# Attention, a mixture of experts and a gated MLP in one kernel: small expert tiles as one stationary block, and engine orders from a second planning pass

## The chip, the cores and the metric

The kernel runs on one core of one Trainium2 chip. The metric is the device time of one execution in microseconds (us). The engines are PE (TensorE, matmuls), DVE (VectorE), ACT (ScalarE), POOL (GpSimd) and SP (the queue that issues most DMAs). PSUM, into which PE writes, has eight banks of 128 x 512 float32.

## The reference

Three stages in a row, all in float32, on 4 sequences of 576 tokens with 512 features (2304 tokens in all):

```
scores = q @ k.T / 8                                   # 32 heads of 576 x 64
attn   = softmax(where(scores >= rowmax - tau, scores, -1e9));  x = attn @ v
# experts: each token goes to one of 8, chosen by x @ w_gate and a local gate
out[b, s] = p[e] * (relu(x[b, s] @ w1[e]) @ w2[e])     # w1[e] 512 x 1024, w2[e] 1024 x 512
# gated MLP
h = gelu(x @ w_in);  u, v = halves of h
v_n = (v - mean(v)) / sqrt(var(v) + 1e-6) * g_ln
out = x + (u * (w_sg @ v_n + b_sg)) @ w_out
```

## The kernel before, in words

**Numbers in two parts.** From the experts on, a float32 operand is held as a high part, rounded to the type that PE takes at full speed, and a low part, the rest. A product is three matmuls: high x high, high x low, low x high. ACT writes the high part as a copy, DVE the low part as a difference.

**The expert stage** (`Tail.moe`). A first expert's first two tiles of 128 tokens come ahead (`plain`); then a loop over eight slots (`CAPS`, `SLOTS`) runs one expert each. Slot 0 has 272 tokens, slots 1 to 3 have 352, slot 4 has 240, and slots 5 to 7 have 192. For each slot SP loads eight pieces of weights of 512 KB; ACT (`whi`) and DVE (`wlo`) split them. The first layer (`L1`) has the weights stationary and the slot's tokens moving: eight groups of 12 matmuls. Relu gives the hidden layer, whose high part `hh` comes from ACT and low part `hl` from DVE. In the second layer (`second`, `L2`) a tile of 128 tokens of the hidden layer is stationary and the weights move, 512 columns at a time: 8 pieces x 3 products = 24 matmuls of 128x512 a tile. A slot's last tile may be a small one: 16 tokens in slot 0, 96 in slots 1 to 3, 112 in slot 4, 64 in slots 5 to 7. It takes 24 matmuls all the same. `put` copies the sum out of PSUM on ACT (`ysb`) and stores it to the DRAM tensor `ys` (`yst`).

**The end of the expert stage.** The small tile of slot 6 is held back: after slot 7's first tile come slot 6's small tile and slot 7's small tile, 48 matmuls. The MLP's first half (`p` = 0) gathers its tokens from `ys` with indirect DMAs on POOL's queue (`gth`). These wait for all stores but those of the last two small tiles.

**The MLP** (`Tail.mlp`) runs per half of the tokens: three groups of three tiles (`group`), then gates (`gate`: `sp`, then `fin`). In a group each tile is scaled by its expert's probability (`xpg`: on DVE in the first group, on ACT later), transposed (`xT`), split (`xh` ACT, `xl` DVE) and multiplied (`vp` 12 matmuls of 512 columns, `up` 12 of 384). Gelu alternates ACT and DVE: `sq`, `sqh`, `tanh`, `gelu`; the last one frees the PSUM bank. `bn`/`bna` (DVE) give mean and variance; 1/sqrt is a guess (`rq`, three DVE operations of 128x3) and three Newton steps (`rqn`, 13 POOL operations of 128x3). Then `vc` (DVE), `vh` (ACT) and `vl` (DVE) make the normalized halves that `sp` needs. `shi`/`slo` split the MLP's own weights.

**Who sets the order.** Every operation is recorded with an engine, a duration, the operations that it needs and a priority (`Graph.add`). `Graph.order` plays a greedy list schedule over all engines: on each engine the operation with the lowest (earliest start + priority) goes next. The order that comes out is the program order of each engine, in which every engine then runs strictly. It also picks PSUM banks: of those that are free, the one freed last.

```
k = s + alpha * o.prio
...
o.banks = [max((b for b in range(8) if bank[b] <= s), key=lambda b: (bank[b ^ 1] > s, bank[b]))]
```

From the expert stage on, nearly all instructions carry one line, L193, that of the recording helper; attention's have their own lines (L437 scores, L442 row maximum, L466 mask).

Of the kernel before, what the change touches and what calls it, by code (L numbers as in the profile page):

```python
# [8 lines left out]
F32 = mybir.dt.float32  # L9
# [15 lines left out]
class Op:  # L25
    __slots__ = ("eng", "dur", "deps", "emit", "prio", "start", "end", "n", "name", "need", "cls", "users", "banks", "fill", "lag")

    def __init__(self, eng, dur, prio, emit, name):
        self.eng, self.dur, self.prio, self.emit, self.name = eng, dur, prio, emit, name
        self.need, self.cls, self.users, self.banks, self.fill, self.lag = 0, None, [], None, False, 0.0  # L30


class Graph:
# [11 lines left out]
    GAP = 0.05  # L45

# [6 lines left out]
    def add(self, eng, dur, prio, emit, name, deps=()):  # L53
        o = Op(eng, dur, prio, emit, name)
        o.deps = [d for d in deps if d is not None]
        o.n = len(self.ops)
        self.ops.append(o)
        return o

    def order(self, alpha=1.0, smax=3):  # L60
# [27 lines left out]

        def when(o, f):
# [14 lines left out]
        while left:  # L104
            best = None
            for e, lst in ready.items():
                f = free.get(e, 0.0)
                c = cs = ck = None
                for o in lst:
                    s = when(o, f)  # L110
                    if s >= INF:
                        continue
                    k = s + alpha * o.prio
                    if c is None or (k, o.n) < (ck, c.n):
                        c, cs, ck = o, s, k
# [13 lines left out]
            o.start, o.end = s, s + o.dur + (self.STEP if e == "PE" else 0.0)  # L129
# [25 lines left out]
        return sorted(ops, key=lambda o: (o.start, o.n))  # L155

# [1166 lines left out]
class Tail:  # L1323
# [10 lines left out]
    CLAG = 2.0  # L1334
    IDLE = 0
# [43 lines left out]
    def moe(self, dep, x_dram, ys, side, sw):  # L1379
# [83 lines left out]
        def second(t, hh, hl, W8, hu, T, after=(), W=W, n=2, more=()):  # L1463
            p = Bank()
            for f0 in range(0, 8, n):
# [8 lines left out]
                R["last"] = g.op("PE", pe(512, 3 * n), W(T), mm, r=hu[f0:f0 + n] + (list(more[f0 + 1:f0 + n + 1])) + wc, deps=after, pw=p, name="L2")  # L1474
                R["last"].fill = n == 1
                T += pe(512, 3 * n)
            put(t, p, T)
            return T
# [44 lines left out]
        switch(*Mem.CELLS[3])  # L1523
        base, free, held = NA, [], None
        for k, cap in enumerate(CAPS):
# [18 lines left out]
            H = (self.HH, self.HL)  # L1544
            if k > 5:
                pitch = z
                H = tuple(self.HP + (2 * (k - 6) + i) * 8 * z for i in range(2))
            hh, hl = (self.M(a, [128, 8, pitch], F32R) for a in H)
            hu = [g.use(*[(a + pitch * m, pitch) for a in H]) for m in range(8)]
            if k == 0:  # L1550

                for x in (hh, hl):
                    g.op("POOL", 0.6, W(T + self.PZ), lambda x=x, a=z, b=pitch: nc.gpsimd.memset(x[:, :, a:b].bitcast(F32), 0.0), w=hu, name="half")
            free = []
            for m in range(8):
# [10 lines left out]
                first(m, p, hh, hl, z, hu[m], W(T + 1.3), W(T + 1.6))  # L1566
# [4 lines left out]
            def row(i, t, T, after, hh=hh, hl=hl, W8=W8, hu=hu, H=H, pitch=pitch):  # L1571
                if pitch % 128 and i:
                    flat = [self.M(a, [128, 8 * pitch + 64], F32R) for a in H]
                    x, y = (lambda f, a=a: a[:, f * pitch + 128:f * pitch + 256] for a in flat)
                    return second(t, x, y, W8, hu, T, after, more=hu + (follow if t == NT - 3 else []))
                c = slice(i * 128, (i + 1) * 128)
                return second(t, hh[:, :, c], hl[:, :, c], W8, hu, T, after)
# [4 lines left out]
            elif k == 7:  # L1582
                follow = hu[:1]
# [242 lines left out]
    def mlp(self, out):  # L1826
# [24 lines left out]
        def rsqrt(var2, q):  # L1851
# [17 lines left out]
            return y, guess, newton  # L1869

        def group(p, gi):
# [4 lines left out]
            for n, i in enumerate(turn):  # L1876
# [13 lines left out]
                for (k0, k1), xk in zip(parts[i], xt[i]):  # L1890
# [13 lines left out]
                    else:  # L1904
                        g.op("ACT", act(512), W(need - 4), lambda t=t, y=y: nc.scalar.activation(y, y, AF.Copy, scale=self.pg[p][:, t:t + 1]), r=[xu], w=[xu], deps=first, name="xpg")
# [7 lines left out]
            y, guess, newton = rsqrt(mv, rq)  # L1913
# [43 lines left out]
            g.op("POOL", 3.4, W(T[0] + 3), newton, r=[rq], w=[rq], name="rqn")  # L1957
# [224 lines left out]
```

## Time and profile before

| what | value |
|---|---|
| median of 3 runs | 772.18 us (771.45 to 773.78) |
| profiled execution, its own time | 771.32 us |
| its span in the profile | 769.5 us |
| PE busy | 747.7 us (97%) |
| DVE busy | 610.5 us (79%) |
| ACT busy | 456.4 us (59%) |
| POOL busy | 181.2 us (24%) |
| granted TensorE clock | 0.999 of full speed |

The profiled execution's own time is 1.8 us above its span, which covers first to last instruction. A busy share is an average over stages: attention fills about 0 to 300 us, the experts up to 540 us, the MLP the rest.

### The profile page before, as it was taken

The page shows a single profiled execution, that of the slowest core. Times are in us where ns is not written, and L with a number is a line of the kernel's source. Part 1 is how long each engine was busy: PE and PEld are TensorE (multiplying, and loading weights), DVE is VectorE, ACT ScalarE, POOL GpSimd, SP SyncE. Part 2 cuts the span into 40 slices and gives each one's busy share as a digit, 9 for nine tenths or more (in the row PEclk, how much of TensorE's full clock was granted, in tenths as well). Part 3 has the DMA queues.
Part 4 walks back from the last instruction along what each step waited for, and adds up shares of the span by engine and source line. Part 5 has one row for each costly group of instructions (what it writes and reads, how often), then busy time and mean ns, then how long its engine had stood idle before and what let it go on. Part 6 is the DMA issues. An engine that isn't in the chain of part 4 may idle for free.

```text
span 769.5 us, 13939 instructions
## 1 busy us (share of the span) xinstructions
PE 747.7 (97%) x4885; PEld 646.1 (84%) x4886; DVE 610.5 (79%) x1321; ACT 456.4 (59%) x842; POOL 181.2 (24%) x348
## 2 busy tenths in 40 slices
PE   8999999999999999999999999999899999999997
PEld 5787888788788678889898998998788898988996
DVE  7999999999889999667877868876698864588752
ACT  6888888888888585263544445643665542455410
POOL 6433353433344320320101100002241120122100
PEclk9999999999999999999999999999999999999999
DMA  7442323453231243698759578752710032200012
GB/s 217 134 128 63 127 78 127 167 179 126 78 127 63 91 163 117 202 299 295 244 189 289 175 239 296 235 194 92 207 41 1 1 110 69 70 1 0 15 42 69
DMA packets 46910, 103.13 MB, mean 134 GB/s; under 512 B 7540, under 2 KB 7540, under 8 KB 46836
## 3 DMA queue, kind: packets, MB, share of 16 engines
q1 hardware_dynamic: 43636, 91.72, 35.9%
q0 software_dynamic: 3200, 10.49, 4.6%
q8 instruction: 39, 0.64, 0.4%
q14 instruction: 35, 0.29, 0.1%
HBM read 80.17 MB, written 22.02 MB: 133 GB/s over the span
## 4 chain that ended last, share of the span: by engine, by line
PE 43%; DVE 6%; POOL 3%; ACT 2%; DMA 2%; issue 1%; POOLq 0%; ACTq 0%; DVEq 0%
PE PS L193 43%; DVE MF L193 3%; POOL rq L193 2%; DVE r L193 1%; ACT MF L193 1%; DMA MF<-ys,MF 1%; DVE bs L193 1%; POOL MF L193 1%; ACT r L193 1%; POOL r L193 0%; DVE MR L193 0%; DMA ys<-MF 0%; DMA out_dram<-MF 0%; ACT MR L193 0%; DVE rq L193 0%
## 5 line engine op out<-in xcount | busy, mean ns | idle before, releaser
L193 PE MATMUL PS<-r,r 128*128 128x512 f32 (+4 forms) x1544 | 302.2, 352 | 4.2 <-DVE MF L193 3.1
L193 PEld LDWEIGHTS PS<-r,r 128*128 128x128 f32 x1544 | 256.5, 188 | 35.2 <-DVE MF L193 4.0
L437 PE MATMUL PS<-MR 128*128 128x288 f32 x640 | 123.1, 322 | 5.2 <-DVE MF L466 3.2
L466 DVE SCALAR_TENSOR_TENSOR MF<-PS,MF 128x576 f32<-128x576 f32 x144 | 116.1, 811 | 7.8 <-ACT MF L457 6.1
L457 ACT ACTIVATE MF<-PS,MF 128x576 f32<-128x576 f32 x144 | 106.8, 751 | 16.4 <-DVE MF L442 9.4
L442 DVE TENSOR_REDUCE MF<-PS 128x1 f32<-128x576 f32 x144 | 106.1, 751 | 4.8 <-PE PS L437 3.6
L437 PEld LDWEIGHTS PS<-MR 128*128 128x128 f32 x640 | 93.2, 192 | 13.5 <-DVE MF L466 6.6
L193 PE MATMUL PS<-MR,r 128*128 128x256 f32 (+2 forms) x616 | 101.7, 322 | 0.9 <-DVE MF L193 0.9
L193 PEld LDWEIGHTS PS<-MR,r 128*128 128x128 f32 x616 | 91.3, 188 | 9.6 <-DVE MF L193 1.7
L379 ACT ACTIVATE c<-PS 128x512 f32<-128x512 f32 (+1 forms) x160 | 86.0, 564 | 17.5 <-PE PS L486 16.5
L193 ACT ACTIVATE r<-PS 128x512 fp32r<-128x512 f32 (+7 forms) x113 | 49.4, 451 | 79.0 <-PE PS L193 77.4
L486 PE MATMUL PS<-ident,MF 128*128 128x128 f32 x576 | 84.8, 274 | 2.2 <-ACT c L379 1.3
L193 ACT ACTIVATE MF<-PS 128x512 f32<-128x512 f32 (+1 forms) x64 | 35.7, 558 | 72.7 <-PE PS L193 61.3
L486 PEld LDWEIGHTS PS<-ident,MF 128*128 128x128 f32 x576 | 67.7, 140 | 5.9 <-ACT c L379 3.0
L193 DVE SCALAR_TENSOR_TENSOR MF<-MF,PS 128x384 f32<-128x384 f32 (+1 forms) x84 | 50.0, 605 | 19.0 <-ACT MF L193 18.2
L193 DVE TENSOR_TENSOR r<-c,r 128x1024 fp32r<-128x1024 f32 x46 | 55.2, 1222 | 10.2 <-ACT r L193 9.0
L452 POOL TENSOR_TENSOR MF<-MF,cf 128x1 f32<-128x1 f32 x120 | 28.2, 237 | 136.8 <-DVE MF L442 123.7
L193 POOL DMA_INDIRECT MF<-x_dram,inv x22 | 22.3, 1016 | 145.6 <-PE PS L193 117.0
L193 PE MATMUL PS<-r,MR 128*128 128x256 f32 (+3 forms) x384 | 52.4, 294 | 0.4 <-PEq L1777 0.4
L193 DVE SCALAR_TENSOR_TENSOR r<-PS,r 128x352 fp32r<-128x352 f32 (+4 forms) x72 | 30.7, 436 | 27.5 <-ACT r L193 26.8
L193 PEld LDWEIGHTS PS<-r,MR 128*128 128x128 f32 x384 | 50.7, 189 | 1.1 <-DVEq L1777 0.7
L193 ACT ACTIVATE r<-c 128x1024 fp32r<-128x1024 f32 x46 | 46.8, 1054 | 6.2 <-PE PS L193 5.7
(236 smaller groups left out, 935.5 us busy)
## 6 DMA issues: line engine op xcount, KB each, us to landing
c<-in_w_dram SPq DMA_DIRECT2D x64, 512.0 KB, 5.3
c<-in_kP_dram SPq DMA_DIRECT2D x32, 288.0 KB, 2.9
c<-in_qP_dram SPq DMA_DIRECT2D x32, 288.0 KB, 3.0
ys<-MF SPq DMA_DIRECT2D x36, 256.0 KB, 3.7
x_dram<-c SPq DMA_DIRECT2D x6, 768.0 KB, 4.3
MF<-in_w_in_dram SPq DMA_DIRECT2D x8, 512.0 KB, 4.5
c<-in_vP_dram SPq DMA_DIRECT2D x12, 320.0 KB, 4.6
out_dram<-MF SPq DMA_DIRECT2D x12, 256.0 KB, 2.0
```

The source lines that it names most:

```text
L193: return lambda *a, **k: x(*[v(y) for y in a], **{n: v(y) for n, y in k.items()})
L379: self.nc.scalar.activation(out, src, AF.Copy, **k)
L437: self.nc.tensor.matmul(self.PS[:, banks[hf], 0:288], q, k[:, 288 * hf:288 * hf + 288], start=(n == 0), stop=(n == len(ops) - 1))
L442: self.nc.vector.tensor_reduce(m, self.tl[i]["s"], axis=AX.XY, op=ALU.min)
L452: (self.nc.vector if eng == "DVE" else self.nc.gpsimd).tensor_tensor(self.nbt(i), self.tl[i]["m"], self.tp, op=ALU.add)
L457: self.nc.scalar.activation(e.rearrange("p (a b) -> p a b", a=2), t["s"], AF.Exp, bias=t["m"], scale=-1.0)
L466: self.nc.vector.scalar_tensor_tensor(w.rearrange("p (a b) -> p a b", a=2), t["s"], self.nbt(i), t["e"].rearrange("p (a b) -> p a b", a=2) ...
L486: self.nc.tensor.transpose(p[:, c, :], t["w"][:, z + c * 128:z + (c + 1) * 128], self.cst["ident"])
```

## The change

1. **Small tiles share stationary blocks.** Where the last tile's tokens, rounded up to a multiple of 32, are 64 or fewer (slots 0, 5, 6, 7), the hidden layer is laid out so that the small tile's high and low columns stand side by side (`both`). One stationary block holds high and low; the weights' high and low parts move through it. `narrow` does 16 matmuls a tile in place of 24, low x low now included. The two row groups of the result are added at the end: ACT copies the lower one (`ysb`), DVE adds the upper one (`ysa`, new, one a tile). `hl` of these slots becomes two DVE operations, one for the full tiles and one for the small one.
2. **Two planning passes.** `order` runs the old schedule once (`plan`), takes PE's order from it, gives each operation the latest time by which PE needs it or its bank (`aim`), and plans again. In the second pass PE's order from slot 0 on is fixed, the other engines' key there is the latest time, durations come from a new table (`TIME`), and DVE and POOL operations marked `SHARED` may not overlap. Banks from slot 0 on: the one that has been free longest. Attention keeps its key, but is planned again with the new durations.
3. **Newton steps.** In each half's third group they move from POOL (13 operations) to DVE (10). Elsewhere POOL keeps them and the plan's duration for them rises from 3.4 to 4.85 us. The plan adds 2 us for a gather before `xpg` on ACT (`XPL`).

```diff
+    TIME = {
+        ("ACT", "kh"): 0.668, ("ACT", "qh"): 0.668, ("ACT", "nb"): 0.19, ("ACT", "vh"): 0.663, ("ACT", "xpg"): 0.625,
...
-    def order(self, alpha=1.0, smax=3):
+    def plan(self, alpha=1.0, smax=3, line=None):
...
+        def key(o, s):
+            return s + alpha * o.prio if line is None or o.n < self.n0 or o.eng == "PE" else s + 14.8 + self.BETA * (o.late - o.step - 293.0)
+
         def when(o, f):
+            if line is not None and o.eng == "PE" and o.n >= self.n0 and line[pos[0]] is not o:
+                return INF
             t = max(f, at[o.n])
+            if line is not None and o.port:
+                t = max(t, held["POOL" if o.eng == "DVE" else "DVE"])
...
-                    o.banks = [max((b for b in range(8) if bank[b] <= s), key=lambda b: (bank[b ^ 1] > s, bank[b]))]
+                    can = [b for b in range(8) if bank[b] <= s]
+                    o.banks = [min(can, key=lambda b: bank[b]) if o.n >= self.n0 else max(can, key=lambda b: (bank[b ^ 1] > s, bank[b]))]
...
+    def aim(self, seq):
...
+        for o in reversed(seq):
+            o.late = min(o.late, free.get(o.n, INF), t + 5.0)
+            s = ideal[o.n] if o.eng == "PE" else o.late - o.step
+            for d in o.deps:
+                d.late = min(d.late, s - self.lat(d, o.eng) - o.lag)
+        return [o for o in line if o.n >= self.n0] + [None]
+
+    def order(self, alpha=1.0, smax=3):
+        return self.plan(alpha, smax, self.aim(self.plan(alpha, smax)))
...
+            if q:
+                g.op("DVE", dve(512), W(T), lambda: nc.vector.tensor_tensor(o[0:n], p.ap[0:n], o[0:n], op=ALU.add), w=[yo], r=[yo], pr=p, name="ysa")
...
+        def narrow(t, both, q, W8, hu, T, after):
+
+            p = Bank()
+            for f0 in range(0, 8, 2):
+                wc, wh, wl = W8[4 + f0 // 2]
+
+                def mm(f0=f0, wh=wh, wl=wl):
+                    for f in (f0, f0 + 1):
+                        for j, y in enumerate((wh, wl)):
+                            nc.tensor.matmul(p.ap[0:2 * q], both[:, f, :], y[:, f % 2 * 512:f % 2 * 512 + 512], start=(f == 0 and j == 0), stop=(f == 7 and j == 1))
...
+            full, q = z // 128 * 128, (z % 128 + 31) // 32 * 32
+            if q <= 64:
...
+                for c, hx, lx in ((slice(0, full), slice(0, full), hl), (slice(full, z), slice(0, z - full), both[:, :, q:2 * q] if q else None)):
+                    if c.stop > c.start:
+                        g.op("DVE", dve(c.stop - c.start), W(T + 1.6), lambda m=m, p=p, c=c, hx=hx, lx=lx, hh=hh: nc.vector.scalar_tensor_tensor(
+                            lx[:, m, hx], p.ap[:, c], 0.0, hh[:, m, c].bitcast(F32), op0=ALU.max, op1=ALU.subtract), r=[hu[m]], w=[hu[m]], pr=p, name="hl")
...
-            g.op("POOL", 3.4, W(T[0] + 3), newton, r=[rq], w=[rq], name="rqn")
+            if gi < 2:
+                g.op("POOL", 4.85, W(T[0] + 3), newton, r=[rq], w=[rq], name="rqn")
+            else:
+                g.op("DVE", 1.65, W(T[0] + 3), fast, r=[rq], w=[rq], name="rqd")
```

**PE at the end of the expert stage.** The rows are PE's program order before, from slot 7's last L1 matmuls (192 columns) over the three L2 tiles (512 columns), the MLP's first transposes (`ident`) and the first `vp` matmuls.

```order
L193 MATMUL PS<-r_3193,r_3113 128x192 x3
L193 MATMUL PS<-MR,r_3193 128x512 x24
L193 MATMUL PS<-r_3112,r_3193 128x512 x24
L193 MATMUL PS<-MR,r_3193 128x512 x24
L193 MATMUL PS<-ident,MF 128x128 x12
L193 MATMUL PS<-r_3112,r_3193 128x512 x6
L193 MATMUL PS<-r_2737,r_3193 128x512 x3
```

The same place now:

```order
L256 MATMUL PS<-r_3186,r_3113 128x192 x3
L256 MATMUL PS<-MR,r_3186 128x512 x24
L256 MATMUL PS<-r_3112,r_3186 128x512 x16
L256 MATMUL PS<-MR,r_3186 128x512 x16
L256 MATMUL PS<-ident,MF 128x128 x4
L256 MATMUL PS<-r_3112,r_3186 128x512 x6
L256 MATMUL PS<-ident,MF 128x128 x4
L256 MATMUL PS<-r_2733,r_3186 128x512 x3
```

The two small tiles have 16 matmuls each, and the transposes of the second and third tile now stand between the first `vp` matmuls.

**ACT at the start of the MLP.** Before; `MF<-PS` of 512 or 384 columns is `sq`, `MR<-c` is `shi`, `r<-PS` is `xh`. Of `MF<-MF 128x512` the first two are `xpg` of gathered tiles, then after `sq` one `xpg` and the first `tanh`, then after the next `sq` one `xpg` and the second `tanh`.

```order
L193 ACTIVATE r_3193<-PS 128x4x128 x2
L193 ACTIVATE MF<-MF 128x512 x2
L193 ACTIVATE MF<-PS 128x512
L193 ACTIVATE MF<-MF 128x512 x2
L193 ACTIVATE MR<-c_78 128x576
L193 ACTIVATE MF<-PS 128x512
L193 ACTIVATE MF<-MF 128x512 x2
L193 ACTIVATE MF<-PS 128x384
L193 ACTIVATE MR<-c_79 128x576
L193 ACTIVATE MF<-MF 128x384
```

Now; the second row is `sq`, the third the first `tanh`, and the three in one row are `xpg`, the second `tanh`, `xpg`. The single `MF<-MF 128x512` behind `shi` is the `xpg` that stood just ahead of the second `tanh`.

```order
L256 ACTIVATE r_3186<-PS 128x4x128 x2
L256 ACTIVATE MF<-PS 128x512
L256 ACTIVATE MF<-MF 128x512
L256 ACTIVATE MF<-PS 128x512
L256 ACTIVATE MF<-MF 128x512 x3
L256 ACTIVATE MF<-PS 128x384
L256 ACTIVATE MR<-c_80 128x576
L256 ACTIVATE MF<-MF 128x512
L256 ACTIVATE MF<-MF 128x384
```

Before, all four scalings stood ahead of the second `tanh`; now one does, and the other three follow it.

**DVE behind the guess of the second group, first half.** Before; `rq` is the guess, `MF<-MF,mv` is `vc`, `r<-MF,rq,r` is `vl`, which needs the Newton steps, `MF<-MF,PS` is `sqh` or `gelu`.

```order
L193 TENSOR_SCALAR rq_108<-rqi_109 128x3
L193 SCALAR_TENSOR_TENSOR MF<-MF,PS 128x512
L193 SCALAR_TENSOR_TENSOR MF<-MF,mv_101 128x512 x3
L193 SCALAR_TENSOR_TENSOR r_3193<-MF,rq_108,r_3193 128x512
L193 SCALAR_TENSOR_TENSOR MF<-MF,PS 128x512
L193 BN_STATS bs_97<-MF 128x6
```

Now; `MR<-c` is `slo`.

```order
L256 TENSOR_SCALAR rq_108<-rqi_109 128x3
L256 SCALAR_TENSOR_TENSOR MF<-MF,mv_101 128x512
L256 SCALAR_TENSOR_TENSOR MF<-MF,PS 128x384
L256 SCALAR_TENSOR_TENSOR MF<-MF,mv_101 128x512
L256 TENSOR_TENSOR MR<-c_79,MR 128x576
L256 TENSOR_TENSOR MR<-c_75,MR 128x576
L256 TENSOR_TENSOR MR<-c_77,MR 32x576
L256 SCALAR_TENSOR_TENSOR MF<-MF,PS 128x512
L256 SCALAR_TENSOR_TENSOR r_3186<-MF,rq_108,r_3186 128x512
```

Between guess and first `vl` stand four operations before, and one `gelu`, three `slo`, two `vc` and one `sqh` now.

## Rows read from the trace of the kernel before

**Rows 1.** The profile's page: busy us of each engine, share of span, instructions.

```profile
PE 747.7 (97%) x4885; PEld 646.1 (84%) x4886; DVE 610.5 (79%) x1321; ACT 456.4 (59%) x842; POOL 181.2 (24%) x348
```

**Rows 2.** Stage windows: length, busy us of each engine, granted clock, DMA share, GB/s.

```profile
100.00:200.00 100.00, 99.45 (x748) 82.18 (x749) 94.84 (x206) 85.03 (x164) 41.06 (x74) 1.00 0.41 133
...
450.00:529.00 79.00, 79.00 (x553) 72.68 (x553) 64.50 (x108) 41.25 (x70) 0.95 (x1) 1.00 0.63 213
...
541.00:598.00 57.00, 53.33 (x278) 47.45 (x279) 45.37 (x83) 36.67 (x65) 15.35 (x34) 1.00 0.25 74
...
646.00:705.00 59.00, 58.04 (x299) 50.79 (x298) 40.49 (x75) 30.65 (x54) 11.82 (x31) 1.00 0.13 41
```

**Rows 3.** Timeline of PE, end of the experts: start, us, instruction, idle time before.

```profile
528.68 5.63 PE L193 MATMUL PS<-r,r 128*128 128x512 f32 x24
534.14 5.76 PE L193 MATMUL PS<-MR,r 128*128 128x512 f32 x24
539.74 1.04 PE L193 MATMUL PS<-ident,MF 128*128 128x128 f32 x8
...
541.40 9.93 PE L193 MATMUL PS<-r,r 128*128 128x512 f32 x48
553.48 4.46 PE L193 MATMUL PS<-r,r 128*128 128x384 f32 x24 [2.15 <-DVE MF L193]
```

**Rows 4.** Timeline of POOL, the MLP's first and seventh gather.

```profile
532.77 0.95 POOL L193 DMA_INDIRECT MF<-ys,MF  x1 [70.25 <-DVE r L193]
...
544.19 0.96 POOL L193 DMA_INDIRECT MF<-ys,MF  x1 [0.52 <-issue]
```

**Rows 5.** Timeline of DVE: scaling of the MLP's first three gathered tiles.

```profile
536.13 0.62 DVE L193 TENSOR_SCALAR MF<-MF 128x256 f32<-128x256 f32 x2 [3.95 <-DMA MF<-ys,MF]
538.55 0.53 DVE L193 TENSOR_SCALAR MF<-MF 128x512 f32<-128x512 f32 x1 [1.80 <-DMA MF<-ys,MF]
540.21 0.72 DVE L193 TENSOR_SCALAR MF<-MF 128x512 f32<-128x512 f32 x1 [1.13 <-DMA MF<-ys,MF]
```

**Rows 6.** Timeline of ACT: the scaling of the seventh gather's tile, with `tanh` behind it.

```profile
551.46 1.24 ACT L193 ACTIVATE MF<-MF 128x512 f32<-128x512 f32 x2 [3.69 <-DMA MF<-ys,MF]
```

**Rows 7.** PE's waits, 545 to 615 and 0 to 300: us, times, longest.

```profile
PE PS L193 <- DVE MF L193: 3.4, 5, 2.2
PE PS L193 <- DVE r L193: 1.1, 1, 1.1
...
PE PS L437 <- DVE MF L466: 3.2, 6, 1.3
```

**Rows 8.** Timeline of POOL: Newton steps of the first half's first two groups.

```profile
566.85 0.19 POOL L193 TENSOR_TENSOR rq<-rq 128x3 f32<-128x3 f32 x1 [6.94 <-DVE rq L193]
...
573.78 0.24 POOL L193 TENSOR_SCALAR rq<-rq 128x3 f32<-128x3 f32 x1
588.95 0.20 POOL L193 TENSOR_TENSOR rq<-rq 128x3 f32<-128x3 f32 x1 [14.93 <-DVE rq L193]
...
590.26 0.58 POOL L193 TENSOR_TENSOR rq<-rq,rq 128x3 f32<-128x3 f32 x1
...
593.53 0.23 POOL L193 TENSOR_SCALAR rq<-rq 128x3 f32<-128x3 f32 x1
```

**Rows 9.** Timeline of DVE around the second group's Newton steps.

```profile
588.49 0.17 DVE L193 TENSOR_SCALAR rqi<-rq 128x3 int32<-128x3 int32 x1
...
589.37 2.07 DVE L193 SCALAR_TENSOR_TENSOR MF<-MF,mv 128x512 f32<-128x512 f32 x3
594.54 0.75 DVE L193 SCALAR_TENSOR_TENSOR r<-MF,rq,r 128x512 fp32r<-128x512 f32 x1 [3.10 <-ACT r L193]
```

**Rows 10.** DVE by shape, 300 to 769 us: count, busy us, mean ns, idle before.

```profile
L193 DVE TENSOR_TENSOR MF<-PS,MF 128x512 f32<-128x512 f32 x14 | 9.7, 691 | 13.7 <-PE PS L193 11.6 <-DMA out_dram<-MF 2.0
L193 DVE SCALAR_TENSOR_TENSOR r<-PS,r 128x192 fp32r<-128x192 f32 x24 | 8.5, 356 | 8.0 <-ACT r L193 7.5
...
L193 DVE SCALAR_TENSOR_TENSOR MF<-PS,MF 128x64 f32<-128x64 f32 x16 | 3.4, 215 | 0.0
```

More of the change, by code (lines that the diff above doesn't have):

```diff
@@ L25 @@
 class Op:
-    __slots__ = ("eng", "dur", "deps", "emit", "prio", "start", "end", "n", "name", "need", "cls", "users", "banks", "fill", "lag")
+    __slots__ = ("eng", "dur", "deps", "emit", "prio", "start", "end", "n", "name", "need", "cls", "users", "banks", "fill", "lag", "late", "port", "step")
     def __init__(self, eng, dur, prio, emit, name):
@@ L45 @@
     GAP = 0.05
+    BETA = 0.06
+    n0 = 1 << 30
+    TIME = {
+        ("ACT", "kh"): 0.668, ("ACT", "qh"): 0.668, ("ACT", "nb"): 0.19, ("ACT", "vh"): 0.663, ("ACT", "xpg"): 0.625,
+        ("DVE", "mask"): 0.739, ("DVE", "bn"): 0.714, ("DVE", "bna"): 0.147, ("DVE", "la"): 0.464, ("DVE", "rd"): 0.098,
+        ("DVE", "slo"): 1.135, ("DVE", "wlo"): 1.135, ("POOL", "nb"): 0.256, ("POOL", "half"): 0.786, ("POOL", "gth"): 0.982,
+        ("PE", "av"): 2.466, ("PE", "tr"): 0.42, ("PE", "xT"): 0.36,
+    }
+    SHARED = dict(
+        DVE={"rqd", "rq", "wlo", "slo", "vc", "vl", "gl", "kh", "qh", "kl", "ql", "rt", "rc"},
+        POOL={"kl", "ql", "cv", "slo", "gl", "half", "rows", "rc"},
+    )
     def __init__(self):
@@ L128, in order @@
             ready[e].remove(o)
-            o.start, o.end = s, s + o.dur + (self.STEP if e == "PE" else 0.0)
+            o.start, o.end = s, s + (o.dur if line is None else o.step) + (self.STEP if e == "PE" else 0.0)
+            if line is not None:
+                pos[0] += e == "PE" and o.n >= self.n0
+                if o.port:
+                    held[e] = o.end - 0.06
             free[e] = o.end
@@ L155, in order @@
         return sorted(ops, key=lambda o: (o.start, o.n))
+    def aim(self, seq):
+        INF = 1e18
+        line = [o for o in seq if o.eng == "PE"]
+        t, ideal = line[0].start, {}
+        for o in line:
+            ideal[o.n] = t
+            t += o.step + self.STEP
+        for o in seq:
+            o.late = INF
+        last = {}
+        free = {}
+        for o in line:
+            for b in o.banks or ():
+                if b in last:
+                    for x in last[b].users:
+                        free[x.n] = min(free.get(x.n, INF), ideal[o.n] - self.lat(x, "PE"))
+                last[b] = o
+        for o in reversed(seq):
[6 more added lines that the diff above has]
+        return self.plan(alpha, smax, self.aim(self.plan(alpha, smax)))
 class Later:
@@ L1334 @@
     CLAG = 2.0
+    XPL = 2.0
     IDLE = 0
@@ L1472, in mm @@
                             nc.tensor.matmul(p.ap, x(f) if callable(x) else x[:, f, :], y[:, s], start=(f == 0 and i == 0), stop=(f == 7 and i == 2))
[L1474 removed]
+                R["last"] = g.op("PE", pe(512, 3 * n), W(T), mm, r=hu[f0:f0 + n] + wc, deps=after, pw=p, name="L2")
                 R["last"].fill = n == 1
@@ L1570, in moe, with row @@
                 self.rt.turn.deps += free
[L1571 to L1575, printed above, removed]
+            def row(i, t, T, after, hh=hh, hl=hl, both=both, W8=W8, hu=hu, full=full, q=q):
+                if 128 * i == full:
+                    return narrow(t, both, q, W8, hu, T, after)
                 c = slice(i * 128, (i + 1) * 128)
@@ L1867, in newton, with fast @@
                 nc.gpsimd.tensor_scalar(y, y, 0.5, None, op0=ALU.mult)
-            return y, guess, newton
+            def fast():
+                for k in range(3):
+                    v.tensor_tensor(z, y, y, op=ALU.mult)
+                    v.scalar_tensor_tensor(z, z, -0.5, a, op0=ALU.mult, op1=ALU.mult)
+                    v.scalar_tensor_tensor(y, z, 1.5, y, op0=ALU.add, op1=ALU.mult)
+                v.tensor_scalar(y, y, 0.5, None, op0=ALU.mult)
+            return y, guess, newton, fast
         def group(p, gi):
```

52 lines of the change are left out of this document (35 added, 17 removed).

## The prediction

> **What bounds the kernel now.** I read the page's busy shares first, then the stage windows, then PE's timeline and waits at the places that the change touches. PE is busy 747.7 of 769.5 us [rows 1], and the granted clock is 1.00 in every window, the 2.4 GHz level [rows 2]. The windows show why the share alone misleads: in the expert stage PE is busy 79.00 of 79.00 us while DVE has 64.50 and ACT 41.25, so there every matmul removed is time; in 541 to 598 PE is busy 53.33 of 57.00, and 3.7 us of idle stand among work that DVE and ACT feed; in attention PE has 99.45 and DVE 94.84 of 100 us, two full engines with no room on either [rows 2].
>
> A busy PE need not be at its peak, so I check its pace. The held small tile's 24 matmuls start at 528.68 and the next 24 at 534.14: 0.2275 us each; the next 24 last until 539.74, 0.233 each [rows 3]. I use 0.23.
>
> **Matmuls removed.** Four small tiles (slots 0, 5, 6, 7) go from 24 to 16 matmuls, 32 fewer in all: 32 x 0.23 = 7.4 us. The bounds are narrow, 7.3 and 7.5 by the two paces. Their weight loads go with them. What could eat the gain is DVE, which now has two `hl` where it had one. One of 192 columns took 0.356 us and a comparable one of 64 columns 0.215 [rows 10]; one of 128 lies between, I take 0.29 by its size. So 0.15 more for each of 24 in slots 5 to 7, 3.6 us, some 1.5 us in slot 0, and four `ysa` of 0.69 [rows 10]. In 450 to 529 DVE would have 64.5 + 3.6 + 0.7 = 68.8 us in a stretch of 77: 89%, still beside PE, at no cost. Were that cover gone, the 4 us would come out of the 7.4.
>
> **Less cover at the start of the MLP.** The MLP's gathers wait for slot 7's first tile, not for the two small ones. Counted in the times of before, PE is through with 32 matmuls 7.4 us after 528.68, at 536.1 and not 539.74: 3.7 us earlier. The gathers stay: the first is issued at 532.77 [rows 4], and the three tiles are scaled by 536.75, 539.08 and 540.93 [rows 5]. From the first transpose (539.74) to the first `vp` (541.40) it took 1.7 us [rows 3]. So `vp` can start at 536.75 + 1.7 = 538.4, 3.0 earlier than now; its 12 matmuls last to 541.2, the second tile is there by 540.8, `up` would start at 543.9, and the third tile is ready by 542.6. PE's order rows agree: the later transposes stand between the `vp`. Of the 3.7 us 0.7 is lost. Bounds: 0, or the whole 3.7 if the gathers' tiles hold PE as they do now.
>
> **Stalls in the MLP.** PE waits 2.15 us before 553.48 [rows 3]. The chain: the seventh gather, issued at 544.19 behind POOL's memsets [rows 4], lets ACT stand 3.69 us until 551.46, with the second `tanh` behind it [rows 6]; without `tanh` no `gelu` on DVE, without `gelu` no free bank. Now that `tanh` goes ahead of it, only the third waits, and PE takes the bank that has been free longest, so that it can run several accumulations ahead of an unfinished `gelu`. I take the whole 2.15. The rest of PE's waits between 545 and 615 is 3.4 + 1.1 - 2.15 = 2.35 us [rows 7]. DVE stood 3.10 us before 594.54, when the Newton steps on POOL lasted from 588.95 to 593.76 [rows 8, 9], and what it owed then came late. The new order puts one `gelu`, three `slo` and one `sqh` there. I take half of the 2.35, 1.2 us. In the second half PE idles 59.00 - 58.04 = 0.96 us [rows 2]; I take 0.3. Together 3.7 us. Bounds: nothing, and all of 5.5.
>
> **Newton on DVE.** Ten operations where POOL had 13. The nearest row is the guess's, 0.17 us [rows 9], so 1.7 us; at POOL's 4.81 / 13 = 0.37 it would be 3.7. What waits for them is the third group's `vl`, needed only by later gates, so the shorter chain gives nothing by itself. DVE's load in 541 to 598 is 45.37 of 57.00 [rows 2]; in 52 us with 2 us more it is 91%. It is hidden; without that cover it costs 2 us in each half.
>
> **Attention.** Nothing is removed, but all engines are planned again. The longest item of PE's waits there is 3.2 us for masks [rows 7]. I take 0, with 3.2 either way as bounds, since the moves are by a few places and both engines are full. SP's loads keep their order but for a few places, at a DMA share of 0.63 in the expert stage [rows 2]: 0.
>
> **The sum.** The profiled execution took 771.3 us by its own time: 771.3 - 7.4 + 0.7 - 3.7 = 760.9. The median of the runs is 0.9 higher, so 761.8; I say 762.
>
> **Rivals.**
> (a) The MLP's start stays nailed to the gathers. For it: the tiles' times don't hang on PE [rows 4, 5], and the third `tanh` is still behind the seventh gather, which lands no earlier [rows 6]. Against it: eight banks. Then the 3.7 us are lost and the 2.15 stall stays: 762 + 3.0 + 2.15 = 767.
> (b) Newton again. A step took 0.20 us alone and 0.58 at 590.26, while DVE ran three `vc` from 589.37 to 591.44 [rows 8, 9]; with DVE busy throughout, the first group's steps lasted from 566.85 to 574.02, 7.2 us [rows 8]. The new order fills DVE exactly behind the guess, so the second group's would take 7.2 and not 4.8, beyond the 4.85 planned; `vh` and `vl` are then late for the first gate and its order behind them too: 2.4 us, 764.4. The Trainium skill ("SBUF — State Buffer", Who interferes with whom) has a rule behind this: a DVE instruction with two SBUF inputs and a GpSimd instruction that reads SBUF exclude each other, and the loser waits for the whole instruction. The trace agrees in the slow step beside `vc`, 0.58 against 0.20. By that rule the steps left on POOL are slowed by each `slo` put beside them.
> (c) Slower: attention loses its rhythm. It has 144 score tiles, each with a maximum and a mask on DVE, which is 94.84% busy [rows 2]. If a mask that comes late costs each tile more than (762 to 774.5) 12.5 / 144 = 0.087 us, the kernel ends slower by over 0.3%; at 0.1 us it is 776. For it: the priorities there were made for the old durations. Against it: small moves.
> (d) Attention gains: the masks come earlier and the 3.2 us go: 759.
> (e) The change doesn't give what it says in the experts. Either DVE's 89% is uneven and late `hl` hold PE, or PE is held there by weight loads and not by columns: 553 loads were busy 72.68 of 79 us, 0.131 each [rows 2], so 32 fewer would give 4.2 us and not 7.4. Either way some 765. Against it: the pace of 0.23 is far above 0.131, and PE never stood still there. The Trainium skill ("Perfetto Trace Analysis", Identifying the Most-Contended Engine) says that matmul busy time is no measure of how near TensorE is to its limit and that weight-load busy time is; by it the 92% here, and not PE's 100%, is the number to judge by. The trace agrees that both are high, and doesn't tell which binds.
>
> **How the numbers follow.** The measurement can tell about 0.3%, 2.3 us, from no change: 769.9 to 774.5. Chances: forecast 0.54 (759.5 to 764), (a) 0.13, (b) 0.10, (c) 0.07, (d) 0.08, (e) 0.08. The range 757.5 to 768 holds the forecast with its bounds, (a), (b), (d), (e), and leaves out (c) and mixtures of (a) with losses in attention. Faster 0.87: all but (c) and part of (a) and (e); same 0.07: those and a mild (c); slower 0.06.
>
> **What would show it.** PE has 32 matmuls fewer, and the last two small tiles last 3.7 us each. PE's wait for a bank early in the MLP is under 0.5 us. From the end of slot 7's first tile to the first `vp` it is 10 us and not 12.7. The second group's Newton steps take under 5 us, and DVE has no 3 us hole behind the guess. Attention's windows show PE and DVE as before, and the experts' start doesn't move by more than 3 us. I am wrong if PE shows new idle time among the experts, if the first half's stalls stay above 3 us, or if the experts start later by over 5.

## The result, and the profile after

The changed kernel takes 760.27 us (median of 5 runs, 759.93 to 761.72) against 772.18 us (5 runs, 771.45 to 773.78): ratio 0.9844, 95% interval 0.9831 to 0.9856. That is 11.9 us less, where the forecast said 10.2 (762 us). The profiled execution took 760.27 us by its own time, with a span of 758.5; its end came 11.1 us earlier than that of before. The change gave what it was forecast to give, by way of two errors that partly cancel: the stalls that went were worth twice my price, and attention lost 3 us that I had priced at nothing.

The profile's page, engines after; the row to set it beside is [rows 1].

```profile
PE 741.6 (98%) x4854; PEld 640.2 (84%) x4854; DVE 611.4 (81%) x1377; ACT 456.4 (60%) x842; POOL 176.8 (23%) x323
```

PE is busy 6.1 us less, yet 11 us were won: the removed work shows here (32 weight loads fewer, and 31 of the 32 matmuls in these records), most of the stalls that went do not. Stage windows after, moved along with the work; they answer to [rows 2] one by one.

```profile
100.00:200.00 100.00, 99.48 (x734) 80.29 (x732) 92.23 (x202) 83.14 (x161) 39.07 (x71) 1.00 0.41 133
448.00:527.00 79.00, 79.00 (x555) 72.84 (x554) 72.75 (x144) 43.13 (x71) 0.94 (x1) 1.00 0.70 235
536.40:590.80 54.40, 53.91 (x285) 48.32 (x286) 41.63 (x79) 33.54 (x62) 18.20 (x37) 1.00 0.29 93
637.00:695.00 58.00, 58.00 (x302) 51.67 (x301) 37.71 (x71) 28.62 (x52) 11.59 (x31) 1.00 0.15 42
```

In the experts PE is still busy all the time. In the MLP's first half its idle time fell from 3.67 to 0.49 us, in the second from 0.96 to nothing. Attention's row hides its loss: busy 99.48 of 100 us as before, but 734 matmuls where there were 748. DVE has 92.23 us there and not 94.84, which the sign "DVE as before" had not foreseen.

PE's timeline at the end of the experts, after. It answers to [rows 3]: slot 7's first tile ends at 527.53 (before 528.68).

```profile
527.53 3.81 PE L256 MATMUL PS<-r,r 128*128 128x512 f32 x16
531.18 3.90 PE L256 MATMUL PS<-MR,r 128*128 128x512 f32 x16
535.05 0.70 PE L256 MATMUL PS<-ident,MF 128*128 128x128 f32 x4
536.22 1.99 PE L256 MATMUL PS<-r,r 128*128 128x512 f32 x6 [0.47 <-issue]
538.05 0.60 PE L256 MATMUL PS<-ident,MF 128*128 128x128 f32 x4
538.40 1.64 PE L256 MATMUL PS<-r,r 128*128 128x512 f32 x6
539.88 0.60 PE L256 MATMUL PS<-ident,MF 128*128 128x128 f32 x4
540.23 11.35 PE L256 MATMUL PS<-r,r 128*128 128x512 f32 x60
```

The two small tiles take 3.65 and 3.87 us, and the first `vp` starts 8.7 us behind slot 7's first tile (before 12.7, forecast 10). Where PE stood 2.15 us before its 384-column matmuls, 60 matmuls now run in one piece. PE's waits from 536 to 605, all of them (us in total, times, longest), against 3.4 and 1.1 us in [rows 7]:

```profile
PE PS L256 <- issue: 0.5, 1, 0.5
PE PS L256 <- DVE r L256: 0.4, 1, 0.4
PE PS L256 <- DVE MF L256: 0.2, 1, 0.2
```

ACT in the same stretch answers to [rows 6]:

```profile
542.46 0.63 ACT L256 ACTIVATE MF<-MF 128x512 f32<-128x512 f32 x1 [0.86 <-DVE MF L256]
...
543.76 2.11 ACT L256 ACTIVATE MF<-MF 128x512 f32<-128x512 f32 x3
...
549.94 1.14 ACT L256 ACTIVATE MF<-MF 128x512 f32<-128x512 f32 x2 [3.12 <-DMA MF<-ys,MF]
```

ACT still stands over 3 us for the seventh gather. Only, the first `tanh` (542.46) and the second (in the row of three) are through before that, and PE has banks to go on in.

**A ledger of the two traces.** Idle time misses much here, so I take the start of the same PE operation in both traces and note how far the changed kernel is ahead (minus) or behind (plus), and what each stretch added. "Cover" is the time from the MLP's first transpose to its first `up`: there PE has to wait for gathered tiles unless other matmuls lie over the gathers.

| stretch of PE's program | before, us | after, us | gained or lost, us | forecast |
|---|---|---|---|---|
| start of slot 0's first L2 matmul | 332.14 | 335.10 | +2.96 | 0 |
| small tiles of slots 0, 5 and of 6 with 7 | | | -1.88 -1.85 -3.54 = -7.3 | -7.4 |
| the rest of the experts | | | -0.4 | 0 |
| first transpose to first `up` (cover) | 7.24 | 8.02 | +0.8 | +0.7 |
| MLP, first half: start of `up` 0 to start of `up` 3, then to the ninth `vp`, then to `sp` 4 | | | -2.44 -1.36 -1.30 = -5.1 | -3.4 |
| MLP, the rest: first half from `sp` 4 on, then the second half in two parts | | | -0.13 -0.38 -1.53 = -2.0 | -0.3 |
| end of PE's last matmul | 764.61 | 753.54 | -11.1 | -10.4 |

### The profile page after: what moved, and what is told of

Its sections match the earlier page's. It is cut to its first block, busy times and chain, and to the rows that moved or that the text cites. A ratio compares the mean times of both kernels' runs of the same rounds, so it can differ in the third digit from the quotient of the medians.

```text
span 758.5 us, 13898 instructions
## 1 busy us (share of the span) xinstructions
PE 741.6 (98%) x4854; PEld 640.2 (84%) x4854; DVE 611.4 (81%) x1377; ACT 456.4 (60%) x842; POOL 176.8 (23%) x323
## 4 chain that ended last, share of the span: by engine, by line
PE 43%; DVE 7%; DMA 2%; ACT 1%; POOL 1%; issue 1%; DVEq 0%; POOLq 0%; ACTq 0%
PE PS L256 43%; DVE MF L256 3%; DVE r L256 3%; POOL rq L256 1%; DMA MF<-ys,MF 1%; ACT MF L256 1%; DVE MR L256 1%; ACT r L256 1%; DMA ys<-MF 1%; DMA out_dram<-MF 0%; DVE bs L256 0%; POOL MF L256 0%; DVE rq L256 0%; DVE mv L256 0%; DVE rqi L256 0%
## 5 line engine op out<-in xcount | busy, mean ns | idle before, releaser
L256 PE MATMUL PS<-r,r 128*128 128x512 f32 (+4 forms) x1520 | 296.0, 351 | 1.1 <-issue 0.5
L256 PEld LDWEIGHTS PS<-r,r 128*128 128x128 f32 x1520 | 251.2, 188 | 31.5 <-DVE r L256 1.4
L256 PE MATMUL PS<-MR,r 128*128 128x320 f32 (+2 forms) x608 | 98.9, 321 | 0.2 <-DVE MF L256 0.2
L256 PEld LDWEIGHTS PS<-MR,r 128*128 128x128 f32 x608 | 89.6, 188 | 7.8 <-DVE MF L256 0.4
L256 ACT ACTIVATE MF<-PS 128x512 f32<-128x512 f32 (+3 forms) x64 | 35.3, 556 | 53.4 <-PE PS L256 45.3
L256 POOL DMA_INDIRECT MF<-x_dram,inv x22 | 24.0, 1091 | 141.7 <-PE PS L256 114.0
L256 DVE SCALAR_TENSOR_TENSOR r<-PS,r 128x128 fp32r<-128x128 f32 (+4 forms) x104 | 32.8, 346 | 24.8 <-ACT r L256 22.6
## 6 DMA issues: line engine op xcount, KB each, us to landing
x_dram<-c SPq DMA_DIRECT2D x6, 768.0 KB
```

Of the source, the lines that this page charges most:

```text
L256: return lambda *a, **k: x(*[v(y) for y in a], **{n: v(y) for n, y in k.items()})
```

## The experiments

The theory to test had three parts: 32 matmuls at 0.23 us, a new order at the MLP's start that keeps most of that gain, and stalls that go with the banks and the earlier `tanh`. Its rivals were the MLP's start nailed to the gathers (a), slow Newton steps (b), and, once the result was there, what had slowed attention. Each kernel differs from the changed one by the edit shown, long ones cut to their core. All ratios are to the kernel before.

**1. The small tiles alone.** One planning pass, the old bank rule, Newton steps all on POOL.

```diff
...
-        return self.plan(alpha, smax, self.aim(self.plan(alpha, smax)))
+        return self.plan(alpha, smax)
...
-    XPL = 2.0
+    XPL = 0.0
...
-            if gi < 2:
-                g.op("POOL", 4.85, W(T[0] + 3), newton, r=[rq], w=[rq], name="rqn")
+            if gi < 3:
+                g.op("POOL", 3.4, W(T[0] + 3), newton, r=[rq], w=[rq], name="rqn")
```

> The small tiles' shared blocks with the old planning: one pass, old durations, old bank choice, Newton steps all on POOL. Theory A (the removed matmuls are worth their pace, attention's loss and the MLP's gain both belong to the planning): attention as before, so 772.2 - 7.4 + 0.7 to 3.7 at the start of the MLP = 765.5 to 768.5, with a stall of 2 to 6 us at the MLP's third up. Rival (the small tiles' layout by itself costs attention or DVE something): above 769.

Measured 767.07 us (766.03 to 768.1), ratio 0.9935 [0.9922, 0.9949]. The ledger has the tiles at -1.85, -1.85 and -3.38, attention at +0.3, and a loss of 3.47 us between the MLP's first transpose and its first `up`. PE's timeline there shows where:

```profile
532.72 0.41 PE L256 MATMUL PS<-ident,MF 128*128 128x128 f32 x2
534.63 0.44 PE L256 MATMUL PS<-ident,MF 128*128 128x128 f32 x2 [1.50 <-DVE r L256]
...
538.37 0.66 PE L256 MATMUL PS<-ident,MF 128*128 128x128 f32 x4 [1.90 <-DVE MF L256]
...
549.53 2.71 PE L256 MATMUL PS<-r,r 128*128 128x384 f32 x14 [1.74 <-DVE MF L256]
```

So rival (a) is what the small tiles meet under the old planning: the last two tiles' gain is waited away for the gathered tiles, and the stall at `up` stays.

**2. The planning alone.** The expert stage of before, with 24 matmuls for each small tile, under the new planning.

```diff
-        def narrow(t, both, q, W8, hu, T, after):
...
-                for c, hx, lx in ((slice(0, full), slice(0, full), hl), (slice(full, z), slice(0, z - full), both[:, :, q:2 * q] if q else None)):
```

> The two-pass planning, the bank choice and the Newton steps on DVE, with the experts' small tiles at 24 matmuls as before. Theory A: attention loses 2.9 us, the MLP gains 7, so 772.2 - 4 = 768.1 (767 to 769.5). Rival (the planning's gain hangs on the shorter small tiles, or the small tiles' gain on the planning): outside that; if the two changes helped each other, this and the small tiles alone would together save under 10 of the 11.9 us.

Measured 768.0 us (766.58 to 768.52), 0.9942 [0.9929, 0.9956]. Attention loses 3.7 us, the cover 0.6 (the time from the MLP's first transpose to its first `up`); the MLP wins -2.45 at `up`, -0.71 and -1.38 on the way to the first gate, -1.77 in it, then -0.38 and -1.53. Beside 772.05 us for the kernel before in the same runs, the two halves alone save 5.0 and 4.05 us, 9.0 together, and the whole change 11.9. The two parts help each other at the cover, which costs 3.47 + 0.60 us in the halves and 0.8 in the change. That does not explain the 2.9 by itself: behind the MLP's first `up` the halves win 1.2 and 8.3 us, together 2.3 more than the 7.2 of the change. In the traces PE ends 4.7 and 4.4 us earlier in the halves, 2.0 less than the 11.1 of the change, and half of these 2.0 is attention, whose loss differed by 0.7 us between executions.

**3. The old bank rule, everything else as changed.**

```diff
-                    o.banks = [min(can, key=lambda b: bank[b]) if o.n >= self.n0 else max(can, key=lambda b: (bank[b ^ 1] > s, bank[b]))]
+                    o.banks = [max(can, key=lambda b: (bank[b ^ 1] > s, bank[b]))]
```

> The changed kernel with the old choice of PSUM bank, the one freed last, in the experts and the MLP. Theory A (the early stall of 2.2 us in the MLP went because tanh and gelu come earlier): 760.3 to 761.3. Rival (it went because PE has more banks to run ahead in): the stall comes back, 762.5 to 765.

Measured 763.32 us (762.42 to 764.05), 0.9887 [0.9872, 0.9902]. The stall is back at its place in PE's timeline:

```profile
541.18 9.27 PE L256 MATMUL PS<-r,r 128*128 128x512 f32 x48
552.18 2.37 PE L256 MATMUL PS<-r,r 128*128 128x384 f32 x12 [1.73 <-DVE MF L256]
```

From `up` 0 to 3 this kernel wins 0.55 us where the change wins 2.44. The bank that has been free longest is worth 1.9 us there, 3 us in the medians. The first two `tanh` are early in this kernel too (542.38 and by 546.2, ahead of the seventh gather), so the earlier `tanh` alone does not take the stall away; whether the bank rule would do it without the earlier `tanh` was not tested. The other stalls do not hang on the bank rule: from `up` 3 to `sp` 4 this kernel wins 3.6 us where the change wins 2.7, and 2.0 behind, as the change does.

**4. The key of before in the second pass.** PE's fixed order, durations and banks stay. The new key is not the latest time alone: it is the earliest start plus 0.06 (`BETA`) times the latest start, where the old one adds the hand-made priority to the earliest start.

```diff
-            return s + alpha * o.prio if line is None or o.n < self.n0 or o.eng == "PE" else s + 14.8 + self.BETA * (o.late - o.step - 293.0)
+            return s + alpha * o.prio
```

> The changed kernel, but the second pass orders the other engines by the old key (earliest start + hand-made priority) instead of the latest time; durations, port rule, bank choice, fixed PE order stay. Theory A (the MLP's gain comes from the bank choice and from honest durations, the gathers' and the Newton steps' among them): within 1 us of 760.3. Rival (it comes from the latest times): the MLP's stalls come back by half or more, 762.5 to 766.

Measured 772.55 us (770.71 to 775.0, 11 runs), 1.0008 [0.9994, 1.0022]. My expectation was 12 us off. The loss against the change is spread over the program: 1.8 us from attention's end to the MLP's first transpose, 1.2 from `up` 3 to the ninth `vp`, 3.4 in the first gate, 2.6 up to the second half, 3.2 behind. PE's waits from 515 to 610 in this kernel:

```profile
PE PS L256 <- DVE r L256: 3.5, 3, 2.0
PE PS L256 <- DVE MF L256: 1.8, 1, 1.8
PE PS L256 <- ACT r L256: 0.5, 1, 0.5
```

With the new banks, durations and PE's fixed order the planning's gain thus hangs on the new key. The 12 us are not what the key is worth by itself: this kernel is 5.5 us slower than experiment 1, which has one pass and none of the new rules, so the old key loses under the fixed order more than the second pass wins. The old key with PE's order free was not run, and the new durations and the rule on DVE and POOL were not tested apart behind attention.

**5. PE's order not fixed.** The counterpart: the other engines keep the latest time, PE's operations go by start and priority.

```diff
-            if line is not None and o.eng == "PE" and o.n >= self.n0 and line[pos[0]] is not o:
-                return INF
```

> The second pass no longer fixes PE's order from slot 0 on: PE's operations go by start and priority again, the other engines still by the latest time. PE's order then differs in four places of the MLP (one transpose, one vp, two fin). Theory: the latest-time key of the other engines is what takes the stalls away, and the fixed order gives nothing of its own: 760.3 within 1.2 us. Rival: the fixed order is needed, since the latest times were worked out for it: 763 or more, lost in the MLP.

Measured 759.95 us (759.5 to 761.12), 0.984 [0.9825, 0.9856]. Fixing PE's order gives nothing of its own; from attention's end on this execution is even 1.2 us ahead of the change (-15.2 against -14.0).

**6. Newton steps all on POOL.**

```diff
-            if gi < 2:
+            if gi < 3:
                 g.op("POOL", 4.85, W(T[0] + 3), newton, r=[rq], w=[rq], name="rqn")
```

> The third group's Newton steps go back to POOL, planned with 4.85 us; everything else as in the change. My prediction priced this part of the change at nothing: then 760.3 within 1 us. Rival: the longer chain makes the third group's normalized halves late for later gates, some 2 us in each half: 762.5 to 764.5, with new idle time of PE before a gate's matmuls.

Measured 760.58 us (760.05 to 762.9), 0.985 [0.9831, 0.9868]. From attention's end on the ledger has -14.03 us against -13.96 of the change. Moving them is worth nothing, as priced.

**7. Attention's order of before, first with both rules off, then with its old durations alone.** The two edits, one for each kernel:

```diff
+        for o in self.ops[:self.n0]:
+            o.step, o.port = o.dur, False
```

```diff
+        for o in self.ops[:self.n0]:
+            o.step = o.dur
```

> The changed kernel, but attention's operations keep the old durations and no port rule in the second pass, so that every engine's order there is that of before. Theory A (attention's 2.9 us come from its new order): 760.3 - 2.9 = 757.4, and the first L2 of slot 0 starts near 332 us. Rival (the 2.9 us are a difference between executions, such as a late start): 760.3 and no difference.

> The changed kernel, attention planned with its old durations but with the port rule between DVE and POOL. Two rec stand behind a qk here. Theory A: 14 x 0.235 = 3.3 us less than the changed kernel, 757.0. Rival (the port rule is what hurts attention): 760 or more.

Measured 757.16 us (756.38 to 757.63), 0.9804 [0.9791, 0.9818], and 756.28 us (756.11 to 756.64), 0.9798 [0.9784, 0.9811]. In both, attention is back at the pace of before (-0.4 us at score tile 126, where the change has +3.32), and the gain behind it is that of the change within 0.9 us. So the loss of 3 us comes with the order that the new durations make, not with the rule on DVE and POOL. The second of these is the fastest kernel of the study, 4 us ahead of the change.

**8. `rec` not behind a score matmul.** `av` is the matmul that makes attention's result; ACT copies it, and a group of six matmuls of 146 columns, `rec` ("reciprocal matmul" in the expectations), multiplies the copy by a constant matrix that unpacks two heads and makes the terms of the experts' gate. In the change 16 of 24 follow directly on score matmuls, before it 4 did, and there the starts lie further apart. I took it for a cost of that succession.

```diff
...
+                    if line is not None and e == "PE" and o.name[0] == "rec" and was[0] == "qk":
+                        k += 0.3
...
```

The second kernel puts this rule on top of the first of experiment 7.

> The changed kernel with one rule more in the second pass: on PE the small float32 matmuls that undo the head packing (rec) are put off while the last operation was a score tile (qk). None of 24 stands behind a qk then, 16 did. Theory A (a rec behind a qk costs 0.235 us more on PE than behind a transpose, and that is attention's loss): 16 x 0.235 = 3.8 us, so 756.5 (755.8 to 757.5), with attention's other new order kept. Rival (the loss comes from DVE's and ACT's new order, and the place of rec is beside the point): 760.3 +- 0.7.

> Attention's old order (e3) and the rule that no rec stands behind a qk (four did). Theory A: 757.2 - 4 x 0.235 = 756.2. Rival: 757.2.

Measured 759.82 us (759.12 to 760.35), 0.9844 [0.983, 0.9857], and 757.89 us (757.66 to 758.15), 0.9818 [0.9804, 0.9831]. Theory A failed both times: the first time lies in its rival's range, the second 0.7 us above its rival's. The groups now run at full pace, but from score tile 54 to 126 PE still needs 136.9 us (change 136.85, before 134.26): another wait has come up. PE's waits from 100 to 300, the costliest row in this kernel, and that of the same statement in the fastest one:

```profile
PE PS L593 <- ACT c L447: 1.9, 5, 0.8
```

```profile
PE PS L590 <- ACT c L444: 0.6, 3, 0.2
```

`av` waits 1.9 us for ACT's copies of transposed probabilities, where it waited 0.6. That is at most 1.3 of the 2.6 us; the rest is not traced row by row.

**9. Which duration.** Only the score matmuls planned 10% longer, the other durations of attention as before; and the reverse.

```diff
+        for o in ops[:self.n0]:
+            if o.name[0] != "qk":
+                o.step = o.dur
```

```diff
+        for o in ops[:self.n0]:
+            if o.name[0] == "qk":
+                o.step = o.dur
```

> In the second pass attention is planned with the old durations, but for the score matmuls, which keep their 10% longer plan; everything else as in the change. 19 of the 24 reciprocal matmuls then stand right behind a score matmul on PE. Theory A: it is this one entry that costs attention its 3 us; then PE's start-to-start time from score tile 54 to 126 is about 136.9 us and not 134.2, and the kernel takes 759.5 to 761. Theory B: it is the mask's shorter plan, or all entries together; then attention runs as before the change (134.2 to 134.8) and the kernel takes 756.3 to 757.5.

> The counterpart: all new durations stay in attention, but the score matmuls have their old one; 9 of 24 reciprocal matmuls stand behind a score matmul. Theory A: attention's loss goes for the most part, tile 54 to 126 takes 134.2 to 135 us and the kernel 756.3 to 757.8. Theory B: the loss stays, 136.5 to 137, and the kernel takes 759.5 to 761.

Measured 764.6 us (763.78 to 765.03), 0.9896 [0.9881, 0.991], and 762.72 us (762.48 to 762.99), 0.9872 [0.9856, 0.9888]. Neither theory holds: the longer score alone costs more than the whole set of durations, and taking it out makes attention worse too (tile 126 at +7.8 and +6.8 us). So the loss does not belong to the score's entry; the others were not tried one by one. In these two kernels PE also waits longer for masks, 4.3 and 5.1 us (3.2 in [rows 7]).

## Why the prediction was right, point by point

**Matmuls removed: right.** Forecast -7.4, measured -7.3, tile by tile at 0.23 us for each of the 32. DVE's two `hl` took 0.288 and 0.217 us (forecast 0.29 and 0.215). DVE rose to 72.75 of 79 us in the experts (forecast 68.8 of 77): the two `hl` and `ysa` added the 4 us of the forecast, and the new order moved some 4 us of other work there. PE did not stand still, so rival (e) is out. Its 92% and its 0.131 us a load were averages over two kinds of work. Before the change, the loads were busy all the time in the first layer of slot 7 (192 columns), but 4.12 of 5.00 us, 82%, in the held small tile (512 columns), from where matmuls were taken:

```profile
512.50:523.00 10.50, 10.50 (x97) 10.50 (x96) 6.90 (x16) 2.92 (x8) 0.00 (x0) 1.00 0.43 151
529.00:534.00 5.00, 5.00 (x24) 4.12 (x23) 3.14 (x4) 0.47 (x1) 0.95 (x1) 1.00 0.28 107
```

The Trainium skill ("Perfetto Trace Analysis", Identifying the Most-Contended Engine) names weight-load busy time as a measure of how near TensorE is to its limit. The 7.3 us do not speak against it, since at this place the loads had room. The traces agree with its other half, that matmul busy time measures little: attention's two rows of 99.45 and 99.48 us hold 748 and 734 matmuls.

**Cover: right in size, partly by luck, and only with the planning.** Forecast +0.7, measured +0.8. The first `vp` came 1.0 us earlier than forecast (8.7 us behind slot 7's first tile and not 9.7), but from it to the first `up` PE took 6.85 us where the forecast had 5.5. The gathers themselves come closer together than I assumed: the first three tiles are scaled 7.7, 9.1 and 10.4 us behind slot 7's first tile, by these rows of DVE; in [rows 5] it was 8.1, 10.4 and 12.3.

```profile
534.63 0.62 DVE L256 TENSOR_SCALAR MF<-MF 128x256 f32<-128x256 f32 x2 [1.94 <-DMA MF<-ys,MF]
536.14 0.49 DVE L256 TENSOR_SCALAR MF<-MF 128x512 f32<-128x512 f32 x1 [0.88 <-DMA MF<-ys,MF]
...
537.49 0.49 DVE L256 TENSOR_SCALAR MF<-MF 128x512 f32<-128x512 f32 x1 [0.20 <-issue]
```

Rival (a) is real: under the old planning it took 3.5 us (experiment 1).

**Stalls: right mechanism, wrong size.** Forecast -3.7 with an upper bound of 5.5; measured -7.1. The steps that were mis-sized are "I take half of the 2.35" and "in the second half ... I take 0.3": nearly everything went, -1.36 and -1.30 up to `sp` 4 and -2.0 behind. The bound itself was too low, since I added up idle times. The stall of 2.15 us idle cost 2.32 us from start to start beyond the pace of its neighbours, the one of 0.38 cost 0.54 and the one of 0.94 cost 1.10: the end that the profile gives the matmul before a stall lies 0.16 to 0.17 us inside it. Over the seven stalls of before that is 1.1 us; the rest of the difference is not traced to single matmuls. The bank rule carries the first stall (experiment 3). The others went with the second pass under either bank rule and not without it (experiment 1), nor with the old key in it (experiment 4); I had named the order of `tanh` first.

**Newton: right at 0 (experiment 6); rival (b) half seen.** The second group's steps on POOL, first to last:

```profile
581.68 0.62 POOL L256 TENSOR_TENSOR rq<-rq 128x3 f32<-128x3 f32 x1 [13.58 <-DVE rq L256]
582.37 0.19 POOL L256 TENSOR_TENSOR rq<-rq,rq 128x3 f32<-128x3 f32 x1
582.65 0.77 POOL L256 TENSOR_SCALAR rq<-rq 128x3 f32<-128x3 f32 x1
...
587.29 0.23 POOL L256 TENSOR_SCALAR rq<-rq 128x3 f32<-128x3 f32 x1
```

They last 5.84 us: not under 5, as I had it, nor the rival's 7.2. DVE stands 2.10 us before the first `vl`, where it stood 3.10 [rows 9]:

```profile
581.50 0.74 DVE L256 SCALAR_TENSOR_TENSOR MF<-MF,mv 128x512 f32<-128x512 f32 x1
582.16 0.55 DVE L256 SCALAR_TENSOR_TENSOR MF<-MF,PS 128x384 f32<-128x384 f32 x1
582.62 0.75 DVE L256 SCALAR_TENSOR_TENSOR MF<-MF,mv 128x512 f32<-128x512 f32 x1
583.29 2.20 DVE L256 TENSOR_TENSOR MR<-c,MR 128x576 fp32r<-128x576 f32 x3
585.52 0.69 DVE L256 SCALAR_TENSOR_TENSOR MF<-MF,PS 128x512 f32<-128x512 f32 x1
588.31 0.75 DVE L256 SCALAR_TENSOR_TENSOR r<-MF,rq,r 128x512 fp32r<-128x512 f32 x1 [2.10 <-ACT r L256]
```

The work that DVE owed was done by then, and the first gate gains 1.30 us all the same: the longer steps cost PE at most the 0.2 us that it still waits there. The long steps (0.58 to 0.77 us against 0.19) lie between 581.7 and 585.6, beside `vc` and `slo` on DVE; the one at 582.37 lies beside a `gelu`, which reads PSUM, and takes 0.19, and from 585.63 on each takes 0.19 to 0.23. The Trainium skill ("SBUF — State Buffer", Who interferes with whom) says that a DVE instruction with two SBUF inputs and a GpSimd instruction that reads SBUF shut each other out; the trace agrees, with 0.77 us for the third step, beside `vc` and `slo`, against 0.20 for the same step of the next round, beside `gelu`.

**Attention: wrong.** Forecast 0, measured +2.96. The failed step is "I take 0 ... since the moves are by a few places". That it stayed within the bound of 3.2 is luck: the change and experiments 2 to 6 have one order of PE in attention, and they start slot 0's first L2 matmul 2.96 to 3.71 us late. The loss of pace itself repeats: from score tile 54 to 126 these six take 136.81 to 136.88 us, three with the order of before (the kernel before, experiment 1, the first of experiment 7) 134.24 to 134.29. Rival (c) had the side right but not the mechanism: not late masks. One `rec` group in the change, on PE and on ACT; `MF<-PS 128x288` on ACT copies the result of `av` that `rec` multiplies.

```profile
112.10 0.75 PE L590 MATMUL PS<-c,c 128*128 128x288 f32 x2
112.48 0.91 PE L500 MATMUL PS<-MR 128*128 128x288 f32 x4
113.36 1.01 PE L603 MATMUL PS<-MF 128*128 128x146 f32 x6
114.20 0.60 PE L549 MATMUL PS<-ident,MF 128*128 128x128 f32 x4
```

```profile
112.89 0.41 ACT L597 ACTIVATE MF<-PS 128x288 f32<-128x288 f32 x1
```

The same group in the fastest kernel, whose attention runs at the pace of before:

```profile
111.01 0.75 PE L592 MATMUL PS<-c,c 128*128 128x288 f32 x2
111.39 0.90 PE L502 MATMUL PS<-MR 128*128 128x288 f32 x4
112.13 0.60 PE L551 MATMUL PS<-ident,MF 128*128 128x128 f32 x4
112.56 0.91 PE L605 MATMUL PS<-MF 128*128 128x146 f32 x6
113.31 0.38 PE L574 MATMUL PS<-ident,MF 128*128 128x128 f32 x2
```

```profile
111.92 0.44 ACT L599 ACTIVATE MF<-PS 128x288 f32<-128x288 f32 x1
```

Between `av` and `rec` the change has four score matmuls, the other four score matmuls and four transposes. So the copy ends at 113.30 and `rec` starts at 113.36, while the copy of the other ends 0.2 us ahead. The four scores then take 0.88 us from start to start and not 0.74, the group 0.84 and not 0.75: 0.23 us. In the change 15 of 24 groups start 0.05 us behind the end of their copy, before it one did. Thirteen of them lie between score tiles 18 and 126: 13 x 0.23 = 3.0, and PE loses 3.05 us there. Neither the idle column nor the list of waits shows any of it. So these waits make up the loss in the change, but they need not be its cause: experiment 8 set other work ahead of `rec`, those waits went, the pace stayed at 136.9 us, and PE waited for ACT's other copies instead. What delays them with these durations stays open; experiment 9 shows only that the score matmuls' entry alone, and the others without it, each give an order that is worse still.

**The sum.** -7.4 + 0.7 - 3.7 + 0 was forecast, -7.3 + 0.8 - 7.1 + 3.0 - 0.4 came, in the profile.

## What to carry to other kernels

Matmuls taken from a stretch where PE never waits are time, but what stands behind that stretch may have been hidden by them: here half of the gain (3.5 of 7.1 us) was waited away at the next stage's start until the order there was new too. Where PE is "99% busy" compare the same operations' start times in two traces; the busy share and the list of waits missed 3 us that came in pieces of 0.23. And plan again only those stages that are to change, since an order that happens to fit is lost by replanning: attention's time varied by over 8 us among orders made by the same planner from slightly different durations.

## What the runs showed of the hardware that I had not expected

A short wait cost more than itself here. Where a `rec` matmul waited for ACT, its start came 0.26 to 0.28 us behind the one before (0.13 without a wait), and its second matmul again 0.228 us later (0.125 without): 0.13 of wait and 0.10 of pace that is not got back, seen at 14 groups in the change.

DVE's scalings of 128x576 in attention took up to three times as long beside POOL. The edits of the two kernels of experiment 7 differ only in the rule that, in the plan, DVE and POOL operations marked `SHARED` may not overlap in attention. Without it (first row) 15 scalings took 0.78 us on average, with it (second row) 0.51:

```profile
L457 DVE TENSOR_SCALAR MR<-c,cf 128x576 fp32r<-128x576 f32 x15 | 11.6, 775 | 0.0
L457 DVE TENSOR_SCALAR MR<-c,cf 128x576 fp32r<-128x576 f32 x15 | 7.7, 513 | 0.0
```

The seven long ones, 0.82 to 1.55 us, are those that ran beside POOL's differences of 64x576 (`MR<-c,MR`); the other eight took 0.51 to 0.52. The slowest, and what POOL did beside it:

```profile
76.52 1.55 DVE L457 TENSOR_SCALAR MR<-c,cf 128x576 fp32r<-128x576 f32 x1
76.33 1.43 POOL L470 TENSOR_TENSOR MR<-c,MR 64x576 fp32r<-64x576 f32 x1 [0.53 <-ACT MR L455]
```

So the rule frees 3.9 us of DVE; the medians of the two kernels, 757.16 and 756.28 us, lie too close to tell what that is worth to the whole.
